# Masks of seven attention pairs put into PSUM by ScalarE copies instead of TensorE products, with PSUM banks of their own for scores

## Chip, core and metric

The kernel runs on one core of a Trainium2 chip. The metric is the device time of one execution in microseconds (us), as the median of several runs. PE is the matmul engine (TensorE), PEld its weight loads, DVE is VectorE, ACT is ScalarE, POOL is GpSimd, SP the engine that issues nearly all DMAs.

## What is computed

Windowed attention, then a gated layer, then a soft mixture of experts, all in float32. The change touches the attention alone, and there the mask:

```python
scores = scale * np.matmul(q, k.transpose(0, 1, 3, 2))      # 4 batches, 8 heads, 576 positions, 64 wide
mask_plain = (rel >= 0) & (rel < 32)                        # heads 0 to 3
mask_dil = (rel >= 0) & (rel < 128) & (rel % 4 == 0)        # heads 4 to 7
scores = np.where(masks, scores, -1e9)
attn = softmax(scores);  x = attn @ v                       # then x to (2304, 512)
x = (sigmoid(x @ w_gate) * (x @ w_val)) @ w_out             # 512 -> 1536 -> 512
...                                                         # dispatch, 8 experts, combine
```

## The kernel before

**Units and pairs.** Attention is cut into 20 units, four pairs of heads for each of five blocks of tokens (blocks 0 to 3 have 512 tokens, block 4 has 256). The four units of block 0 are done at the start (`first_attn`). The other 16 are done two at a time, as pairs 0 to 7 of the class `Pairs`, between the products of the gated layer (`l1`, matmul at L526) for blocks 0 and 1. A "half" is one call of the inner loop of `l1`: 12 matmuls of 128x512 into one bank. `Pairs` is called once after every half; `SCORES_AT` says after which half the scores of a pair are issued (1, 8, 15, 22, 27, 32, 37, 41), `TURN` how many halves later its two units are turned, and `SUMS_AT` when the weighted sums follow.

**One pair.** `scores` takes two PSUM banks. In each, one matmul of an identity with the mask (bf16, `mask_at`, L139, 128x512) opens the accumulation and writes 0 or a large negative number in every place; 128 small matmuls (L144, 64x64, in all four 32-row strips) then add query times key to it. `softmax` reads the banks on DVE (L355 maxima, L359 or L367 differences), takes exponentials on ACT, sums on DVE, and scales on POOL (L387). `turn` transposes each unit on PE (`tr`, L187) and ACT copies it to SBUF (L188). `sums` makes 128 small products with the values (L207).

**PSUM.** Eight banks: two for `l1` (`ps_l1`), two for small things (`ps_m`), four in the pool `ps_a`, handed out in turn under one tag "a": score banks, turned units (`tr`), turned output weights (`wt_ps`, L467), turned gates (`tp` in `Post.turn`, L815), and later others. A tile waits until the reader of the tile four places earlier in the ring is done.

**Order.** `tc.keep_in_program_order` (`kept`) holds instructions in the written order; for the others a planner chooses the order on each engine. Every engine takes its own queue in order. The queries and keys of pair p+1 are loaded by SP after the scores of pair p; for pair 7 the load goes into the buffers in which the units of pair 6 (block 4) keep their probabilities, so it follows their turns.

Of the kernel before, what the change touches and what calls it, by code (L numbers as in the profile page):

```python
# [17 lines left out]
P = 128  # L18
# [13 lines left out]
C0 = 21  # L32
SCORES_AT = (1, 8, 15, 22, 27, 32, 37, 41)
TURN = 4
SUMS_AT = (10, 17, 25, 29, 34, 39, 44, 47)
C1 = 19
WP = 1
ND = 4
# [21 lines left out]
def tile_kernel(  # L60
# [16 lines left out]
    ps_l1 = ctx.enter_context(tc.tile_pool(name="ps_l1", bufs=2, space=PSUM))  # L77
    ps_a = ctx.enter_context(tc.tile_pool(name="ps_a", bufs=4, space=PSUM))
    ps_m = ctx.enter_context(tc.tile_pool(name="ps_m", bufs=2, space=PSUM))

    BUFS = {
        "xa": 2, "xb": 2, "ga": 3, "gb": 3, "w": 2, "l2": 2,
# [39 lines left out]

    def keep_busy(count):
        if "ps" not in busy:
            busy["ps"] = ps_a.tile([P, 512], F32, tag="a", name="busy")
        for _ in range(count):
            kept(
                nc.tensor.matmul(
                    busy["ps"], lhsT=msk[:, M_ID:M_COLS], rhs=msk[:, 0:512], start=True, stop=True, skip_group_check=True
                )  # L130
            )
# [21 lines left out]
    def scores(u, ts):  # L153
        n, hp = u["id"]
        if "s_ps" not in u:
            u["s_ps"] = [ps_a.tile([P, 4, 64], F32, tag="a", name=f"s_ps{r}") for r in range(2)]
            for r in range(2):
                mask_at(u["s_ps"][r].rearrange("p t c -> p (t c)"), mask[:, 1 if hp >= 2 else 0])
        for t in ts:
            for i in range(4):  # L160
                for r in range(2):
                    score(u, t, i, r, u["s_ps"][r][32 * i : 32 * i + 32, t, :])
# [19 lines left out]

    def turn_unit(u, pool, tag, at=lambda x: x):
        s = u["s"].rearrange("p (c x) -> p c x", c=4)
        tr = pool.tile([P, 4, P], F32, tag=tag, name="tr")
        for c in range(4):
            at(nc.tensor.transpose(tr[:, c], s[:, c], ident))  # L187
        nc.scalar.copy(pt_ring[:, u["z"] % 4].rearrange("p c i q -> p c (i q)"), tr)  # L188
# [105 lines left out]
    class Pairs:  # L294


        def __init__(self):
            self.jobs = [(n, hp) for n in range(1, 5) for hp in HP_ORDER]
            self.us, self.qk, self.v = unit_loads(self.jobs, ["qk"] * 16)
            self.todo = []  # L300
            for p in range(8):
                t = SCORES_AT[p]
                late = t + TURN + (p == 0)
                self.todo += [(t, self.scores, p), (late, self.turn, 2 * p), (late + 1, self.turn, 2 * p + 1)]
                self.todo += [(SUMS_AT[p], self.sums, p)]
            self.todo.sort(key=lambda x: x[0])
            self.n = 0

        def __call__(self):
# [8 lines left out]
                what(2 * p + 1)  # L318

        def turn(self, z):  # L320
            turn_unit(self.us[z], ps_a, "a", kept)

        def scores(self, p):
            two = self.us[2 * p : 2 * p + 2]
            n = two[0]["id"][0]
            bank = [ps_a.tile([P, 512], F32, tag="a", name=f"s_ps{r}") for r in range(2)]
            for r in range(2):
                m_ = mask[:, 0:2] if n < 4 else mask[:, 2:3].to_broadcast([P, 2, 256])
                kept(mask_at(bank[r].rearrange("p (u c) -> p u c", u=2), m_))
            for y, u in enumerate(two):  # L330
                for t in range(4):
                    for i in range(4):
                        for r in range(2):
                            to = bank[r].rearrange("p (u t c) -> p u t c", u=2, t=4)
                            kept(score(u, t, i, r, to[32 * i : 32 * i + 32, y, t]))
            self.softmax(two, bank)
            self.load(self.qk, p + 1)
            if p == 0:
                self.load(self.v, 1)
# [82 lines left out]
    def store():  # L422
        while stores:
            ld(nc.sync.dma_start(*stores.pop(0)))
# [34 lines left out]
    def slot_weights(f, wo_f, lag):  # L459

        wt = pm.rearrange("p a b -> p (a b)").rearrange("p (k c x) -> p k c x", k=ND, c=2)
        at_ = {}

        def turned(c):
            wt_ps = ps_a.tile([P, ND, P], F32, tag="a", name="wt_ps")
            for kc in range(ND):
                nc.tensor.transpose(wt_ps[:, kc], wo_f[:, c, P * kc : P * kc + P], ident)  # L467
            nc.scalar.copy(wt[:, :, c], wt_ps)

        def product():  # L470
            pt_ps = ps_m.tile([P, 2, P], F32, tag="m", name="pt_ps")
            for kc in range(ND):
                nc.tensor.matmul(
                    pt_ps[32 * kc : 32 * kc + 32], lhsT=phi[:, kc, :], rhs=wt[:, kc], start=True, stop=True
                )
            at_["pt"] = cpool.tile([P, 2, P], F32, tag="pt", name="pt")
            nc.vector.tensor_copy(at_["pt"], pt_ps)
# [182 lines left out]
    def pair_l1(f, prev, follow):  # L660
# [14 lines left out]
        tm = b8("l2", [P, 3, 512], F32, "tm")  # L675
        m1, u2, e5 = (tm[:, z] for z in range(3))
        pn = ps_l1.tile([P, 512], F32, tag="l1", name="pa")
        pd = ps_a.tile([P, 512], F32, tag="a", name="pd")
        pe = ps_a.tile([P, 512], F32, tag="a", name="pe")
        product(pn, w["a11"], "b11", True)  # L680
        kp(nc.scalar.copy(m1, pn))
        if prev:
# [69 lines left out]
    class Post:  # L752
# [52 lines left out]
        def turn(self, q, j):  # L805
            if j == 0:
                if not self.last:
                    self.gt[q] = b8("l2", [P, self.ntt, 512], F32, "gt")
                elif q == 0:
                    ring = b8("w", [P, 2, 2, 512], F32, "gt")  # L810
                    self.gt = {z: ring[:, z % 2] for z in range(3)}
            pool, tag = (ps_l1, "l1") if self.last and j else (ps_a, "a")
            tp = pool.tile([P, 4, P], F32, tag=tag, name="tp")
            for c in range(4):
                nc.tensor.transpose(tp[:, c], g_sb[self.n, 4 * q + c][:, P * j : P * j + P], ident)  # L815
            to = self.gt[q][:, j].rearrange("p (c x) -> p c x", c=4)
# [167 lines left out]
    for f in range(NF):  # L984
        whl = split_w(wst[f // 2][:, f % 2])
        if f % 2:
            load_w(f // 2 + 2)
        l1(1, f, whl, beside)
        if NF + f in wo_at:
            convert(NF + wo_at[NF + f])  # L990
    store()
    early[0] = False
    wst.clear()
# [114 lines left out]
        st_ps.rearrange("p k (e a) -> p k e a", a=4),  # L1108
    )
    keep_busy(2)  # L1110
    h_ps = [ps_a.tile([P, 512], F32, tag="a", name=f"h_ps{h}") for h in range(2)]
    reuse = [None, None, "v", "v", "xb", "xa", "xa", "bd", "ga", "ga", "ga", "gb", "gb", "gb"]
    for e in range(8):
        for h in range(2):
# [49 lines left out]
            ALU.max,  # L1164
        )
    sr = cpool.tile([P, 512], F32R, name="sr")
    so_ps = [ps_a.tile([P, 256], F32, tag="a", name=f"so_ps{dh}") for dh in range(2)]

    def half(dh):
        return so[:, 256 * dh : 256 * dh + 256], sr[:, 256 * dh : 256 * dh + 256]  # L1170
# [30 lines left out]
    def result(dh, z):  # L1201
# [6 lines left out]
        for j in range(0, ntt, 2):  # L1208
            more = k == 4 if dh == 0 else n_op[0] // 2 % 2
            n_op[0] += dh  # L1210
            pool, tag = (ps_a, "a") if more else (ps_l1, "l1")
            op = pool.tile([P, 2, 256], F32, tag=tag, name="op")
            for y in range(2):
                kept(nc.tensor.matmul(op[:, y], lhsT=ct[:, j + y], rhs=sr_, start=True, stop=True))
            if j == 0:
# [134 lines left out]
```

## Time and profile before

| | |
|---|---|
| median of 3 runs | 499.2 us (498.91 to 499.81) |
| profiled execution, its own time | 500.05 us |
| its span from first to last instruction | 498.3 us |
| PE busy / PEld / DVE / ACT / POOL | 94% / 72% / 61% / 49% / 32% |
| chain that ended last, share of PE | 82% |

A busy share says how long an engine had an instruction in flight; for PE, matmuls overlap, so their durations add up to more than the time that they take. The chain follows the last instruction back through what released it. Only time on that chain, or in an idle stretch of the engine that it runs on, can be gained.

### The profile page before, as it was taken

What the parts mean: (1) busy time and instruction counts of PE and PEld (TensorE: products, weight loads), DVE (VectorE), ACT (ScalarE), POOL (GpSimd) and SP (SyncE); (2) the same over time, 40 slices, a digit from 0 to 9 for tenths busy, and PEclk for the clock granted to TensorE, in tenths of its full rate; (3) what the DMA queues carried; (4) which work ended last, traced back from release to release, by engine and by line L of the source; (5) the groups of instructions that cost most, each with busy time, mean ns of one, the idle gap of its engine ahead of it and who ended that gap; (6) DMA issues with size and microseconds to landing.
All of it is one profiled execution on the core that took longest, in us unless ns stands there. A gap on an engine that the chain in (4) does not pass through costs nothing.

```text
span 498.3 us, 12720 instructions
## 1 busy us (share of the span) xinstructions
PE 469.7 (94%) x5470; PEld 357.4 (72%) x5476; DVE 305.7 (61%) x567; ACT 245.4 (49%) x422; POOL 159.8 (32%) x132
## 2 busy tenths in 40 slices
PE   6789999999899999989989999999999999999993
PEld 3467777878677877867547888888887889743552
DVE  3869697976766352652997656656558655541522
ACT  2466576747666453551865554554527544300232
POOL 0243555635283421173144323324312123110100
PEclk9889999999999999999999999999999999999998
DMA  8979899979977401650002201201499886589997
GB/s 331 405 250 343 297 323 321 337 267 364 410 256 234 174 1 50 227 220 1 1 0 85 85 22 64 84 8 78 155 375 422 326 337 244 195 314 369 420 388 219
DMA packets 23785, 112.14 MB, mean 225 GB/s; under 512 B 2352, under 2 KB 7216, under 8 KB 14640
## 3 DMA queue, kind: packets, MB, share of 16 engines
q1 hardware_dynamic: 23408, 111.06, 60.0%
q8 instruction: 43, 0.70, 0.6%
q10 hardware_dynamic: 320, 0.26, 0.2%
q14 instruction: 14, 0.11, 0.1%
HBM read 97.16 MB, written 14.16 MB: 223 GB/s over the span
## 4 chain that ended last, share of the span: by engine, by line
PE 82%; DVE 7%; ACT 3%; DMA 2%; issue 2%; POOL 1%; SPq 0%; DVEq 0%; ACTq 0%; POOLq 0%
PE l1ps L526 31%; PE pa L650 12%; PE pe L650 6%; PE tp L815 4%; PE xp L207 4%; PE so_ps L1175 3%; PE h_ps L1116 3%; PE s_ps L144 3%; PE pd L650 3%; PE sp L846 2%; PE lt_ps L779 2%; DMA qk<-qkv 2%; PE tr L187 2%; PE wt_ps L467 1%; DVE whl L493 1%
## 5 line engine op out<-in xcount | busy, mean ns | idle before, releaser
L526 PE MATMUL l1ps<-x_hi,whl 128*128 128x512 f32 x384 | 129.1, 402 | 2.7 <-ACT x_hi L228 2.0
L526 PEld LDWEIGHTS l1ps<-x_hi,whl 128*128 128x128 f32 x384 | 72.1, 189 | 19.4 <-ACT x_hi L228 2.7
L526 PE MATMUL l1ps<-x_lo,whl 128*128 128x512 f32 x192 | 76.2, 397 | 0.0
L441 POOL TENSOR_TENSOR fw<-fw 128x512 int32<-128x512 int32 x36 | 51.5, 1437 | 72.4 <-DVE fw L440 35.3
L538 DVE TENSOR_TENSOR g<-l1ps,g 128x512 f32<-128x512 f32 (+1 forms) x36 | 21.6, 600 | 32.8 <-PE l1ps L526 31.5
L526 PEld LDWEIGHTS l1ps<-x_lo,whl 128*128 128x128 f32 x192 | 36.5, 190 | 7.3 <-issue 0.4
L526 PE MATMUL l1ps<-x,whl 128*128 128x256 f32 x288 | 37.0, 285 | 0.0
L526 PEld LDWEIGHTS l1ps<-x,whl 128*128 128x128 f32 x288 | 35.3, 191 | 2.0 <-issue 1.7
L536 ACT ACTIVATE g<-l1ps 128x512 f32<-128x512 f32 (+1 forms) x36 | 18.9, 526 | 31.1 <-PE l1ps L526 30.9
L493 POOL TENSOR_TENSOR whl<-w,whl 128x512 fp32r<-128x512 f32 x12 | 15.9, 1327 | 51.4 <-ACT whl L492 39.9
L815 PE MATMUL tp<-cst,g 128*128 128x128 f32 x216 | 29.2, 276 | 0.1
L493 POOL TENSOR_TENSOR whl<-wst,whl 128x512 fp32r<-128x512 f32 x12 | 16.1, 1342 | 39.0 <-ACT whl L492 33.4
L815 PEld LDWEIGHTS tp<-cst,g 128*128 128x128 f32 x216 | 24.0, 140 | 5.6 <-issue 3.3
L438 ACT ACTIVATE fw<-st 128x512 f32<-128x512 f32 x36 | 22.6, 672 | 7.0 <-DMA st<-wd 6.8
L493 DVE TENSOR_TENSOR whl<-fw,whl 128x512 fp32r<-128x512 f32 x24 | 21.4, 897 | 7.5 <-ACT whl L492 7.0
L820 ACT COPY gt<-tp 128x512 f32<-128x512 f32 x27 | 15.6, 582 | 19.1 <-PE tp L815 17.5
L207 PEld LDWEIGHTS xp<-pt_ring,v 64*64 64x64 f32 x1216 | 19.7, 137 | 6.1 <-issue 4.5
L440 DVE TENSOR_SCALAR fw<-st 128x512 int32<-128x512 uint32 x36 | 21.9, 635 | 2.8 <-DMA st<-wd 2.8
L492 ACT CAST whl<-fw 128x512 fp32r<-128x512 f32 x24 | 14.7, 620 | 17.9 <-POOL fw L441 13.6
L714 DVE TENSOR_TENSOR tm<-pe,tm 128x512 f32<-128x512 f32 x12 | 8.3, 691 | 23.7 <-PE pe L650 23.7
L439 DVE TENSOR_SCALAR fw<-fw 128x512 uint32<-128x512 uint32 x36 | 21.4, 602 | 2.3 <-ACT fw L438 1.8
L207 PE MATMUL xp<-pt_ring,v 64*64 64x32 f32 (+1 forms) x1216 | 21.1, 221 | 1.6 <-issue 0.9
(464 smaller groups left out, 968.2 us busy)
## 6 DMA issues: line engine op xcount, KB each, us to landing
ew<-w SPq DMA_DIRECT2D x32, 1024.0 KB, 8.3
st<-wd SPq DMA_DIRECT2D x18, 1024.0 KB, 9.0
wst<-wg SPq DMA_DIRECT2D x12, 1024.0 KB, 6.8
v<-qkv SPq DMA_DIRECT2D x20, 512.0 KB, 6.4
wg<-fw SPq DMA_DIRECT2D x12, 512.0 KB, 7.6
w<-wg SPq DMA_DIRECT2D x6, 1024.0 KB, 8.3
qk<-qkv SPq DMA_DIRECT2D x10, 576.0 KB, 5.7
qk<-qkv SPq DMA_DIRECT2D x8, 528.0 KB, 4.4
```

What stands on the lines that cost most here:

```text
L207: nc.tensor.matmul(o, lhsT=v[k, t, i, r, :], rhs=p_[k, 2 * r + t, i, 0:nq], start=True, stop=True)
L438: nc.scalar.activation(top, st[:, c, 1].bitcast(F32), AF.Prelu, scale=2.0**-112, alpha=2.0**32)
L439: nc.vector.tensor_scalar(top.bitcast(U32), top.bitcast(U32), 3, None, ALU.logical_shift_left)
L440: nc.vector.tensor_scalar(low.bitcast(I32), st[:, c, 0], 2.0**-29, None, ALU.mult)
L441: nc.gpsimd.tensor_tensor(low.bitcast(I32), top.bitcast(I32), low.bitcast(I32), ALU.add)
L493: (nc.gpsimd if pool[h] else nc.vector).tensor_tensor(whl[:, 1, h], src[:, h], whl[:, 0, h].bitcast(F32), ALU.subtract)
L526: nc.tensor.matmul(pt[:, 0:nt], lhsT=whl[:, w_, a, dc, :], rhs=x_[n][:, dc, :], start=first, stop=(dc == HP_ORDER[-1] and w_ == 1),)
L536: nc.scalar.activation(g, pt[:, 0:nt], AF.Sigmoid)
L538: nc.vector.tensor_tensor(g, pt[:, 0:nt], g, ALU.mult)
L650: nc.tensor.matmul(pt, lhsT=w[:, w_, P * c : P * c + P], rhs=x_[:, c], start=first and c == 0 and w_ == 0 and x_ is hi, stop=c == 1 and w_ ...
L815: nc.tensor.transpose(tp[:, c], g_sb[self.n, 4 * q + c][:, P * j : P * j + P], ident)
L820: nc.scalar.copy(to, tp)
```

## The change

Pair 0 keeps its two mask matmuls. For pairs 1 to 7 a new step `seed` runs two halves (`SEED = 2`) before the scores: it takes the two banks and issues two ACT copies of the mask (bf16 in SBUF) into them; these copies are not held in order. `scores` then only adds its 128 small matmuls. The four banks of `ps_a` become two tags of two banks: "s" for scores, "a" for turned tiles. Up to the end of block 1 (`four[0]` is False) `bank()` always hands out "a"; after that it alternates between both tags, so that four banks go round again. The units of block 0 take "a" and "s" by turns.

```diff
+SEED = 2
+    four = [False]
+    turn_ = [0]
+    def bank(shape, name):
+        turn_[0] += four[0]
+        return ps_a.tile(shape, F32, tag="as"[turn_[0] % 2], name=name, bufs=2)
@@ def scores(u, ts):            # block 0
-            u["s_ps"] = [ps_a.tile([P, 4, 64], F32, tag="a", name=f"s_ps{r}") for r in range(2)]
+            tag = "as"[u["z"] % 2]
+            u["s_ps"] = [ps_a.tile([P, 4, 64], F32, tag=tag, name=f"s_ps{r}", bufs=2) for r in range(2)]
@@ class Pairs
-                self.todo += [(SUMS_AT[p], self.sums, p)]
-            self.todo.sort(key=lambda x: x[0])
+                self.todo += [(SUMS_AT[p], self.sums, p), (t if p == 0 else t - SEED, self.seed, p)]
+            self.todo.sort(key=lambda x: (x[0], x[1] != self.seed))
+        def seed(self, p):
+            n = self.jobs[2 * p][0]
+            self.banks[p] = [ps_a.tile([P, 512], F32, tag="s", name=f"s_ps{r}", bufs=2) for r in range(2)]
+            for r in range(2):
+                to = self.banks[p][r].rearrange("p (u c) -> p u c", u=2)
+                m_ = mask[:, 0:2] if n < 4 else mask[:, 2:3].to_broadcast([P, 2, 256])
+                if p == 0:
+                    kept(mask_at(to, m_))
+                else:
+                    nc.scalar.copy(to, m_)
         def scores(self, p):
-            bank = [ps_a.tile([P, 512], F32, tag="a", name=f"s_ps{r}") for r in range(2)]
-            for r in range(2):
-                m_ = mask[:, 0:2] if n < 4 else mask[:, 2:3].to_broadcast([P, 2, 256])
-                kept(mask_at(bank[r].rearrange("p (u c) -> p u c", u=2), m_))
+            bank = self.banks.pop(p)
...
@@ turn_unit, slot_weights, Post.turn, pair_l1, expert stage: ps_a.tile(.., tag="a") becomes bank(..)
@@ after the last half of block 1
+    four[0] = True
     store()
```

## Rows read from the trace of the kernel before

**Rows 1.** Busy time by stretches: start:end, length, then each engine's busy us (instructions), PE clock, DMA share.

```profile
75.00:100.00 25.00, 25.00 (x355) 20.31 (x354) 22.32 (x36) 17.77 (x28) 15.21 (x11) 1.00 0.96 330
...
50.00:193.00 143.00, 139.71 (x2138) 112.19 (x2139) 98.51 (x165) 85.34 (x132) 68.47 (x52) 1.00 0.73 260
```

**Rows 2.** Waits of PE from 50 to 217 us: total us, times, longest.

```profile
PE s_ps L144 <- issue: 2.4, 2, 1.6
PE tr L187 <- POOL sm L387: 0.7, 1, 0.7
PE l1ps L526 <- ACT g L536: 0.7, 1, 0.7
PE s_ps L144 <- DMA qk<-qkv: 0.6, 1, 0.6
```

**Rows 3.** Instructions on the score banks, 24 to 217 us: duration ns min/median/max, first and last start.

```profile
L139 PE MATMUL s_ps<-msk x15: 379/379/390, 35.6 to 193.5; 128*128 128x512 bf16 x15
...
L367 DVE TENSOR_TENSOR qk<-s_ps,mx x8: 415/415/415, 179.8 to 209.7; 128x256 f32<-128x256 f32 x8
```

**Rows 4.** Timeline of PE at pairs 1 and 6: start us, us, operation.

```profile
56.46 0.39 PE L526 MATMUL l1ps<-x_hi,whl 128*128 128x512 f32 x1
56.69 0.60 PE L139 MATMUL s_ps<-msk 128*128 128x512 bf16 x2
57.23 1.49 PE L144 MATMUL s_ps<-qk 64*32 64x64 f32 x128
...
176.17 0.60 PE L187 MATMUL tr<-cst,sm 128*128 128x128 f32 x4
176.61 0.59 PE L139 MATMUL s_ps<-msk 128*128 128x512 bf16 x2
177.13 1.48 PE L144 MATMUL s_ps<-qk 64*32 64x64 f32 x128
```

**Rows 5.** PE at pair 7, and the transfer on the chain there.

```profile
193.25 0.59 PE L139 MATMUL s_ps<-msk 128*128 128x512 bf16 x2
193.78 2.81 PE L779 MATMUL lt_ps<-g,wp 128*32 128x128 f32 x90
197.17 0.86 PE L144 MATMUL s_ps<-qk 64*32 64x64 f32 x64 [0.58 <-DMA qk<-qkv]
...
193.56 3.57 DMA qk<-qkv
```

**Rows 6.** Event semaphores on PE's queue before L526.

```profile
L526 PEldq EVENT_SEMAPHORE  x2: 51/51/51, 58.5 to 96.9; - x2
```

**Rows 7.** Turned tiles at the end of block 1, on PE and on ACT.

```profile
217.08 0.66 PE L187 MATMUL tr<-cst,qk 128*128 128x128 f32 x4 [1.35 <-POOL qk L387]
217.57 1.04 PE L815 MATMUL tp<-cst,g 128*128 128x128 f32 x8
...
217.77 0.59 ACT L188 COPY pt_ring<-tr 128x512 f32<-128x512 f32 x1 [1.14 <-PE tr L187]
```

**Rows 8.** The two breaks inside scores, counts up to each, and PE's instruction queue.

```profile
129.55 0.33 PE L144 MATMUL s_ps<-qk 64*32 64x64 f32 x11 [1.59 <-issue]
...
154.42 0.31 PE L144 MATMUL s_ps<-qk 64*32 64x64 f32 x7 [0.79 <-issue]
...
0.00:129.53 129.53, 117.24 (x2006) 90.47 (x2009) 97.97 (x174) 74.87 (x119) 56.04 (x45) 0.97 0.90 327
0.00:154.40 154.40, 141.32 (x2388) 109.38 (x2392) 113.39 (x201) 89.63 (x142) 68.66 (x54) 0.98 0.89 322
...
q8 instruction: 43, 0.70, 0.6%
```

**Rows 9.** ACT: groups of copies with mean ns of one, and its longest wait there.

```profile
L492 ACT CAST whl<-fw 128x512 fp32r<-128x512 f32 x22 | 13.5, 620 | 17.4 <-POOL fw L441 13.2 <-PE l1ps L526 4.0
...
L188 ACT COPY pt_ring<-tr 128x512 f32<-128x512 f32 x16 | 9.3, 583 | 5.5 <-PE tr L187 5.5
...
ACT pt_ring L188 <- PE tr L187: 5.5, 4, 3.1
```

More of the change, by code (lines that the diff above doesn't have):

```diff
@@ L124, in keep_busy @@
         if "ps" not in busy:
-            busy["ps"] = ps_a.tile([P, 512], F32, tag="a", name="busy")
+            busy["ps"] = bank([P, 512], "busy")
         for _ in range(count):
@@ L184, in turn_unit @@
         s = u["s"].rearrange("p (c x) -> p c x", c=4)
-        tr = pool.tile([P, 4, P], F32, tag=tag, name="tr")
+        tr = pool.tile([P, 4, P], F32, tag=tag, name="tr") if pool else bank([P, 4, P], "tr")
         for c in range(4):
@@ L304, in __init__ @@
                 self.todo += [(t, self.scores, p), (late, self.turn, 2 * p), (late + 1, self.turn, 2 * p + 1)]
-                self.todo += [(SUMS_AT[p], self.sums, p)]
-            self.todo.sort(key=lambda x: x[0])
+                self.todo += [(SUMS_AT[p], self.sums, p), (t if p == 0 else t - SEED, self.seed, p)]
+            self.todo.sort(key=lambda x: (x[0], x[1] != self.seed))
+            self.banks = {}
             self.n = 0
@@ L320, in turn @@
         def turn(self, z):
-            turn_unit(self.us[z], ps_a, "a", kept)
+            turn_unit(self.us[z], None, None, kept)
+        def seed(self, p):
[8 more added lines that the diff above has]
+                    nc.scalar.copy(to, m_)
         def scores(self, p):
@@ L464, in turned @@
         def turned(c):
-            wt_ps = ps_a.tile([P, ND, P], F32, tag="a", name="wt_ps")
+            wt_ps = bank([P, ND, P], "wt_ps")
             for kc in range(ND):
@@ L677, in pair_l1 @@
         pn = ps_l1.tile([P, 512], F32, tag="l1", name="pa")
-        pd = ps_a.tile([P, 512], F32, tag="a", name="pd")
-        pe = ps_a.tile([P, 512], F32, tag="a", name="pe")
+        pd = bank([P, 512], "pd")
+        pe = bank([P, 512], "pe")
         product(pn, w["a11"], "b11", True)
@@ L811, in turn @@
                     self.gt = {z: ring[:, z % 2] for z in range(3)}
-            pool, tag = (ps_l1, "l1") if self.last and j else (ps_a, "a")
-            tp = pool.tile([P, 4, P], F32, tag=tag, name="tp")
+            shape = [P, 4, P]
+            tp = ps_l1.tile(shape, F32, tag="l1", name="tp") if self.last and j else bank(shape, "tp")
             for c in range(4):
@@ L1110, in tile_kernel @@
     keep_busy(2)
-    h_ps = [ps_a.tile([P, 512], F32, tag="a", name=f"h_ps{h}") for h in range(2)]
+    h_ps = [bank([P, 512], f"h_ps{h}") for h in range(2)]
     reuse = [None, None, "v", "v", "xb", "xa", "xa", "bd", "ga", "ga", "ga", "gb", "gb", "gb"]
@@ L1166, in tile_kernel @@
     sr = cpool.tile([P, 512], F32R, name="sr")
-    so_ps = [ps_a.tile([P, 256], F32, tag="a", name=f"so_ps{dh}") for dh in range(2)]
+    so_ps = [bank([P, 256], f"so_ps{dh}") for dh in range(2)]
     def half(dh):
@@ L1210, in result @@
             n_op[0] += dh
-            pool, tag = (ps_a, "a") if more else (ps_l1, "l1")
-            op = pool.tile([P, 2, 256], F32, tag=tag, name="op")
+            shape = [P, 2, 256]
+            op = bank(shape, "op") if more else ps_l1.tile(shape, F32, tag="l1", name="op")
             for y in range(2):
```

## The prediction

> **What bounds the kernel now.** I read the page first for the chain that ended last: PE holds most of it, and scores and layer products lie on it one after the other. The mask products can only matter where their neighbours are PE work too, so I went to the table by stretches. The change lies between the first scores of a pair and the last, 35 to 217 us. From 50 to 193 us PE is busy 139.7 of 143.0 us, from 75 to 100 us all 25.0, at a granted clock of 1.00, which is the upper level of 2.4 GHz [rows 1]. ACT is busy 85.3 of 143.0 us, so 57.7 are free. The view of waits says what PE's few idle stretches are: twice "issue" inside scores (2.4 us in all), once POOL's scaling ahead of a turn, once a sigmoid that frees a layer bank, once the keys of a pair by DMA, 0.6 to 0.7 us each [rows 2]. Nothing else ends a wait of PE. So in this stage the order on PE is the time, and an instruction taken off PE is worth what it occupies there, unless what follows it is late for another reason. After 217 us the chain goes on through PE, and what is early there starts the later loads early as well.
>
> **What a mask product occupies.** The group of L139 gives 379 ns for one [rows 3]. 12 of these (pairs 1 to 6) would be 4.5 us, but that is the wrong price: the durations overlap. At pair 1 the last layer product starts at 56.46, the masks at 56.69, the scores at 57.23 us [rows 4]. The row of two masks is 0.60 us long; less one duration of 0.38 it leaves 0.22 between their starts. So the two take 0.44, and 0.10 of the 0.54 up to the scores is the change from a full-width product to the small ones. That change does not go away, since the scores then follow a layer product or a turn, which are full-width too. At pair 6 the masks start at 176.61 and the scores at 177.13, 0.52, of the same make [rows 4]. I take 0.44 for each pair; the bound is 0.53, if the change costs nothing behind a turn, and below that nothing. The page "TensorE: Matmul & The Clock Gate" of the Trainium skill, section "Back-to-back issue gap", gives N/2.4 + 2.5 ns, 216 ns for 512 columns. By it the 12 products are 2.6 us, by the group's durations 4.5; the starts in the timeline agree with the page.
>
> Pairs 1 to 6: 6 x 0.44 = **2.6 us** saved (up to 3.2).
>
> **Pair 7 saves nothing.** Its masks run from 193.25 us, then come logits of the finished block as filler, and then PE waits 0.58 us for keys: the transfer starts at 193.56, right after the turn of the first unit of pair 6, and takes 3.57 us, to 197.13 [rows 5]. The turn lies ahead of the masks, so without them the filler ends 0.44 earlier and the wait is 1.0 instead of 0.58. I take 0, bound 0.53.
>
> **What the seeds cost on ACT.** 14 copies of 128x512 from SBUF into PSUM. The trace has none in that direction; the nearest are the casts SBUF to SBUF at 620 ns and the copies PSUM to SBUF at 583 ns [rows 9]. 14 x 0.60 = 8.4 us. ACT's 57.7 idle us hide them, hence cost 0; with that cover gone they would cost up to 8.4. A seed can wait for one thing, DVE's last reading of the same banks for the pair before. The closest case is pair 7: seeds after half 39, scores of pair 6 after half 37; those are read from 179.8 us on by L367, eight in all for pairs 6 and 7 at 0.415 [rows 3]; four end at 181.5, and two halves of 2.8 after the start of the scores at 177.13 it is past 182 [rows 4]. Behind a seed on ACT stand sigmoids and copies of turned units, and PE's banks wait for these.
>
> **The new wait.** The first score of each unit group now waits for ACT, where it used to follow a product of its own engine. The seed is issued two halves ahead: a half is 12 products 0.23 apart [rows 4], 2.76 us, so the copy has 5.5 us for 1.2 us of work, and ACT's longest wait for a turn is 3.1 us [rows 9]. 3.1 + 1.2 fits in 5.5. What remains is bookkeeping: scores already wait for DMA, and an instruction with a second wait gets an event semaphore ahead of it, 51 ns on PE's queue [rows 6]. I take one for each of six pairs, **0.3 us** lost; bounds 0 and 0.6.
>
> **Two banks for turned tiles instead of four.** Three such tiles within about a microsecond now make the third wait for the ACT copy of the first. Along the pairs, turns and turned weights are some halves apart and their copies follow within a microsecond. At the end of block 1 they crowd: a turn at 217.08, then two `tp` from 217.57 on, and the copy of the turn from 217.77 to 218.36 [rows 7]. The second `tp` began about 218.0 (four of the eight transposes later) and can now start at about 218.4: 0.4 us. The same pattern stands once more one half later. Layer products, which are not held in order, can be put ahead, so between 0 and 0.8; I take **0.4 us** lost. From block 1's end on, alternating tags of two banks are a ring of four again: nothing. The same holds for block 0's units, whose score banks alternate in twos as they did. The loads that `scores` issues stay behind the scores.
>
> **The breaks in scores.** PE stops 1.59 us after 117 of 128 products of pair 4, and 0.79 us after 121 of pair 5, with nothing late. Before the first break the rows count 4015 instructions on PE, before the second 4780, 765 apart, three times 255. PE's instructions come in 43 packets of 0.70 MB together, 16.3 KB each [rows 8]; 255 instructions for each is 64 bytes an instruction. So I read these breaks as ends of a packet inside a dense block, where the next had not come. Each pair loses four instructions (two products, two weight loads): at pair 4 the end moves 16 instructions on, to product 125, at pair 5 20, past the last. If the next packet comes at the same clock time as before, what these two pairs save is waited out: 0.9 lost. If the ends fall harmlessly, 2.4 are gained. I take 0, as most dense blocks hold such an end without a break.
>
> **Sum.** -2.6 + 0.3 + 0.4 = -1.9 us. Made against the profiled execution: 500.05 (span 498.3 and 1.75 around it) to 498.15. That execution is 0.85 over the median of the runs, so the median goes from 499.2 to **497.3 us**. With the terms' bounds: at best 6 x 0.53 + 0.53 + 2.4 = 6.1 saved, 493.1; at worst, without a rival, 2.6 - 0.6 - 0.8 - 0.9 = 0.3 saved, 498.9.
>
> **Rivals.** *Something else is late (499.2).* Pair 7 shows the pattern: PE arrives earlier and waits longer. It becomes the rule if the weights for block 0, which pass DMA, ACT, DVE and POOL, are just in time. For it: from 75 to 100 us DMA is at 0.96 and DVE busy 22.3 of 25 [rows 1]. Against it: PE is busy all 25 us there, so nothing came late, and most of that chain is started by PE freeing buffers, so it moves along. It decides once two thirds of the 2.6 are waited out.
>
> *ACT's queue (slower, 500.8).* The copies are free to be placed by the planner. A seed ahead of a sigmoid delays the bank that the half after next needs; of the 2.76 us of a half the read takes about 0.6, so from 2.1 us of lateness on PE stands. An exponential and its table load together with two seeds would reach that. If each of the seven pairs exposes one copy, 7 x 0.6 = 4.2 are lost against 2.6 saved: 500.8; both copies, 505.0. For it: PE already waited once for a sigmoid [rows 2]. Against: ACT has 40% free. The page "TensorE: Matmul & The Clock Gate", "Specifications", says that ScalarE's queue is strictly first in, first out, where TensorE can pull weight loads ahead; this speaks against moving work from PE to ACT. By it no later sigmoid passes a seed that waits. The trace agrees that ACT stands up to 3.1 us at one instruction [rows 9].
>
> *The breaks go (494.9).* The 1.9 and 2.4 more, less what else shifts: 4.3. For it, the wait on the banks ahead of the masks goes, so PE's queue can be filled earlier; against, the end at pair 4 stays inside the scores.
>
> **How the numbers follow.** Forecast as summed 0.52 (its own range 496.0 to 498.9); something else late 0.18; ACT's queue 0.15; breaks gone 0.15. A measurement of this kernel tells about 0.2%, 1.0 us, from no change. Faster: 0.52 less 0.04 for its upper end, the 0.15 of the breaks, and 0.04 of the "late" case: 0.67. Same: 0.14 of the late case, 0.04 of the forecast, 0.01 of ACT's: 0.19. Slower: 0.14. The range leaves out about half of the case of the breaks and a little under half of ACT's: 495.0 to 500.5.
>
> **What the changed profile would show.** L139 keeps two matmuls of pair 0 and eight of block 0. Scores of pairs 1 to 6 start about 0.32 us after the start of the last layer product ahead of them (0.23 and 0.10). Fourteen ACT copies into `s_ps` of about 0.6 us end over 2 us before their scores. The wait for keys at pair 7 grows to about 1.0 us. The `tp` behind a turn near 215 us starts late or behind layer products. From 50 to 193 us the same work is about 2.6 us shorter. I would be wrong if PE shows waits for `s_ps` on ACT, new waits of L526 for a sigmoid or for weights, or breaks by "issue" of another length than 2.4 us in all: each us there shifts the sum by one.

## The result, and the profile after

The changed kernel takes 504.7 us (median of 6 runs, 502.1 to 507.0), the kernel before beside it 499.1 (6 runs): ratio 1.0089, 95% interval 1.0065 to 1.0114. The ratio is worth 4.4 us, the two medians are 5.6 us apart, and the repetition below gives 4.0; I reckon with 4. The kernel is slower, and outside the predicted range of 495.0 to 500.5 us. Its profiled execution is its fastest: 502.09 us, span 499.9, only 1.6 over the span of before, whose profiled execution lies 0.85 us above its median.

First what the edit did where it was made. The score banks in the changed kernel (duration min/median/max in ns, first and last start):

```profile
L345 ACT CAST s_ps<-msk x14: 575/588/610, 44.4 to 181.9; 128x512 f32<-128x512 bf16 x14
...
L147 PE MATMUL s_ps<-msk x1: 379/379/379, 36.3 to 36.3; 128*128 128x512 bf16 x1
...
  ACT s_ps L345: 6.1, 3
```

Fourteen copies of 0.59 us have taken the place of the products; pair 0's one visible product is left. The last row stands under "who waited for it": ACT stood 6.1 us at three of the copies. At pair 1 the scores follow the last layer product by 0.32 us, where 0.77 us lay between them [rows 4]:

```profile
56.72 0.39 PE L547 MATMUL l1ps<-x_hi,whl 128*128 128x512 f32 x1
57.04 1.19 PE L152 MATMUL s_ps<-qk 64*32 64x64 f32 x99
...
129.59 0.31 PE L152 MATMUL s_ps<-qk 64*32 64x64 f32 x5 [2.16 <-issue]
...
216.26 0.66 PE L196 MATMUL tr<-cst,qk 128*128 128x128 f32 x4 [1.73 <-POOL qk L408]
216.75 0.60 PE L836 MATMUL tp<-cst,g 128*128 128x128 f32 x4
217.28 1.04 PE L867 MATMUL sp<-gt,dt 128*32 128x512 f32 x2
218.26 0.66 PE L836 MATMUL tp<-cst,g 128*128 128x128 f32 x4
218.85 1.06 PE L867 MATMUL sp<-gt,dt 128*32 128x512 f32 x6
219.84 0.50 PE L547 MATMUL l1ps<-x_hi,whl 128*128 128x512 f32 x1
```

The same timeline shows two things that were not in the sum. The break inside pair 4's scores is now 2.16 us (1.59 before, [rows 8]; pair 5's is gone). At the end of block 1 the order is another than in [rows 7]: turn, one `tp`, one gather product `sp` (dispatch weights times turned gates), one `tp`, three `sp` (each `sp` counts as two rows here). Before, turn, two `tp` and four `sp` followed one another. Four `sp` side by side, each on 32 columns of the array, took 1.06 us before; now one alone takes 1.04 and the other three again 1.06.

The second `tp` stands apart because it waits for a bank. Its weight load on PE, and the copy on VectorE that reads the first `tp` out of its bank:

```profile
218.26 0.42 PEld L836 LDWEIGHTS tp<-cst,g 128*128 128x128 f32 x4 [0.84 <-DVE gt L839]
...
217.39 0.69 DVE L839 COPY gt<-tp 128x512 f32<-128x512 f32 x1 [2.08 <-PE tp L836]
```

and that copy in the kernel before, where the second `tp` had begun at about 218.0 [rows 7], ahead of it:

```profile
218.21 0.69 DVE L818 COPY gt<-tp 128x512 f32<-128x512 f32 x1 [2.08 <-PE tp L815]
```

PE's waits from 50 to 217 us, to be held against [rows 2]:

```profile
PE s_ps L152 <- issue: 2.2, 1, 2.2
PE tr L196 <- POOL qk L408: 1.7, 1, 1.7
PE dt_ps L846 <- DVE x L424: 0.8, 1, 0.8
PE s_ps L152 <- DMA qk<-qkv: 0.8, 1, 0.8
```

The waits for `x`, and the longer one for POOL's scaling, are both behind pair 7, between 210 and 216 us.

To place the difference, three more names: `wst` is a 1 MB block of layer weights that comes by DMA, `whl` what ACT casts from it for the layer products, and `h_ps` takes the first products of the experts. I counted the starts of layer products on PE's timeline, twelve to a half, and took differences, so that a late or early start of the program drops out. "Fetch" is the start of the packet of the instruction queue nearest to the first load of `wst` for the pair stage (issued at 202.82 us before), "cast" the first cast into `whl` after it, both from that issue on; the last column goes from the last first-layer half to the first product into `h_ps`. All kernels of this study, one profiled execution each, in us:

```
                  half     half     half     fetch   cast    half     half 71
                  2 to 31  31 to 44 44 to 47                 60 to 66 to h_ps
before            110.11   64.19    16.34    -1.9    6.24    10.69    18.62
after             109.87   61.96    19.04    +3.2    7.63    11.08    19.38
after_again       109.71   62.16    19.13    +4.2    7.69    11.49    19.37
banks_only        112.81   63.44    17.81    -1.9    6.53    11.08    20.96
no_masks          108.46   61.87    18.86    +3.1    7.53    11.08    21.06
seeds_kept        108.73   62.14    19.04    +4.4    7.62    11.08    19.37
one_ring          109.01   62.46    19.24    +3.2    7.59    10.77    20.31
one_ring_kept     112.09   62.26    17.82    +3.3    7.72    11.55    18.62
seeds_tail        108.89   62.26    19.16    +3.3    7.73    10.70    18.61
tail_hoisted      109.76   63.47    16.46    -2.0    6.58    11.14    19.37
after_pad         115.06   61.96    17.67    -1.6    6.25    11.08    19.37
one_ring_pad      111.09   62.34    16.35    -2.0    6.24    10.70    18.61
seeds_tail_pad    109.27   61.89    17.81    -2.3    6.36    10.75    18.61
before_less       112.61   63.30    17.62    +3.0    7.52    10.70    18.62
after_late_pad    109.69   62.79    17.80    -2.1    6.40    11.08    19.37
before_late_pad   110.36   63.92    16.36    -2.7    6.27    10.75    18.62
best_no_pad       110.84   62.14    18.18    +4.5    7.78    10.76    18.61
best              112.30   62.78    16.68    -2.1    6.25    12.10    18.62
```

Before against after: 2.5 us are gained up to half 44 (most of it between 31 and 44), 2.7 are lost in the three halves behind it, 0.4 and 0.75 in the last two columns. That is the 1.6 of the spans, with 0.3 from the start. One profile each is little: the first column alone runs from 108.5 to 115.1.

### The profile page after: what moved, and what is told of

It is laid out like the page before. It is cut to its first block, busy times and chain, and to the rows that moved or that the text cites. A ratio compares the mean times of both kernels' runs of the same rounds, so it can differ in the third digit from the quotient of the medians.

```text
span 499.9 us, 12714 instructions
## 1 busy us (share of the span) xinstructions
PE 467.9 (94%) x5456; PEld 355.6 (71%) x5462; DVE 308.9 (62%) x567; ACT 251.8 (50%) x436; POOL 158.1 (32%) x132
## 4 chain that ended last, share of the span: by engine, by line
PE 67%; DVE 6%; ACT 4%; DMA 3%; issue 2%; POOL 1%; SPq 0%; DVEq 0%; ACTq 0%
PE l1ps L547 22%; PE pa L671 12%; PE pe L671 6%; PE tp L836 3%; PE h_ps L1138 3%; PE pd L671 3%; PE sp L867 3%; PE so_ps L1197 2%; PE lt_ps L800 2%; PE xp L216 2%; DMA v<-qkv 1%; PE s_ps L152 1%; PE wt_ps L488 1%; DVE t_hl L574 1%; PE tr L196 1%
## 5 line engine op out<-in xcount | busy, mean ns | idle before, releaser
L460 DVE TENSOR_SCALAR fw<-fw 128x512 uint32<-128x512 uint32 x36 | 22.4, 630 | 3.9 <-ACT fw L459 3.3
L514 DVE TENSOR_TENSOR whl<-fw,whl 128x512 fp32r<-128x512 f32 x24 | 22.8, 963 | 2.8 <-ACT whl L513 2.3
L461 DVE TENSOR_SCALAR fw<-st 128x512 int32<-128x512 uint32 x36 | 20.7, 600 | 2.8 <-DMA st<-wd 2.8
L513 ACT CAST whl<-wst 128x512 fp32r<-128x512 f32 x24 | 14.0, 619 | 15.2 <-PE l1ps L547 7.9
```

The lines of the kernel that those rows point to most:

```text
L460: nc.vector.tensor_scalar(top.bitcast(U32), top.bitcast(U32), 3, None, ALU.logical_shift_left)
L461: nc.vector.tensor_scalar(low.bitcast(I32), st[:, c, 0], 2.0**-29, None, ALU.mult)
L514: (nc.gpsimd if pool[h] else nc.vector).tensor_tensor(whl[:, 1, h], src[:, h], whl[:, 0, h].bitcast(F32), ALU.subtract)
```

## The experiments

Five rounds each, against the kernel before on the same chip, which gave 500.1 to 500.5 us.

**The change again, and its parts.** after_again is the changed kernel unedited.

> The changed kernel once more, for a second profile and to see how far its runs lie apart. Its first runs gave 502.1 to 507.0 us, its profile was of the fastest. All theories: median 503 to 506. The queue theory (the planner puts the copies into ScalarE's queue as soon as it believes the bank free; in the first profile ScalarE stood 6.1 us before three of them) expects ScalarE to stand 4 to 12 us before copies into s_ps again, and TensorE to lose its time between 60 and 110 us. The rival that the two-bank ring of turned tiles costs it expects the loss near turned tiles, after 110 us.

504.2 us, 1.0083 [1.0056, 1.0110]; its profile repeats the table's pattern. The net loss lies behind half 44, and not between 60 and 110 us as the queue theory had it.

banks_only: the banks kept apart, the masks by products as before.

```diff
-                self.todo += [(SUMS_AT[p], self.sums, p), (t if p == 0 else t - SEED, self.seed, p)]
+                self.todo += [(SUMS_AT[p], self.sums, p), (t, self.seed, p)]
...
-                if p == 0:
-                    kept(mask_at(to, m_))
-                else:
-                    nc.scalar.copy(to, m_)
+                kept(mask_at(to, m_))
```

> Masks by products as before, at the time of the scores, but score banks and turned tiles in two tags of two banks. Ring theory: 502 to 505, most of the loss is here. Queue theory: 498.5 to 500.5, no measurable change, since ScalarE has nothing new to do.

505.3 us, 1.0074 [1.0039, 1.0110]: about as the ring theory has it. Without any copy by ScalarE the kernel is about as slow as the whole change.

no_masks: pairs 1 to 7 get no mask, neither product nor copy; each of their score products opens a sum of its own.

```diff
-                else:
-                    nc.scalar.copy(to, m_)
...
-            start=False,
+            start=start,
```

> Pairs 1 to 7 get no mask at all (left out of the computation): neither products nor copies, every score product opens its own accumulation; banks as in the changed kernel. Queue theory: 495.5 to 498, the 2 to 3 us that the products took and nothing lost on ScalarE. Rival, that the planner's new order on VectorE and TensorE (it differs as soon as the products go) costs the time: 501 to 505, as VectorE's order here is nearly that of the changed kernel.

502.8 us, 1.0043 [1.0018, 1.0068]. With the masks gone at no price, still slower than before: something other than the masks' cost is lost.

seeds_kept: the copies are held at their written place in ScalarE's queue (`kept(nc.scalar.copy(to, m_))`).

> The changed kernel with the copies held in the written order, so that they stand two halves ahead of their scores in ScalarE's queue and not right behind the exponential of the pair before. Queue theory: no wait of ScalarE before a copy into s_ps, 496 to 499. Rival (the copies' 8.4 us of ScalarE work themselves, or the planner's order): 502 to 505, as the changed kernel.

503.2 us, 1.0052 [1.0023, 1.0081], 1.0 us under after_again. The two intervals overlap, and the 496 to 499 of the queue theory are missed: the place of the copies is at most a part. The changed kernel's ScalarE, with the planner free to place the copies:

```profile
86.81 0.59 ACT L345 CAST s_ps<-msk 128x512 f32<-128x512 bf16 x1 [2.34 <-DVE sm L380]
87.33 0.68 ACT L459 ACTIVATE fw<-st 128x512 f32<-128x512 f32 x1
88.03 1.28 ACT L395 ACT_TABLE_LOAD   x1
89.33 1.06 ACT L395 ACTIVATE sm<-sm 128x1024 f32<-128x1024 f32 x1
```

and with them held:

```profile
84.64 1.28 ACT L395 ACT_TABLE_LOAD   x1
86.94 1.06 ACT L395 ACTIVATE sm<-sm 128x1024 f32<-128x1024 f32 x1 [1.02 <-DVE sm L380]
```

The copy for the next pair stood ahead of the exponential of this one and waited 2.34 us for VectorE's reading of the same banks. VectorE's last difference (L380) released copy and exponential alike: with the copies free the exponential began 2.5 us after that (89.33, released by 86.81), with the copies held at once (86.94), its table load done during the wait. The sigmoid and the casts of layer weights queued behind it are late with it. Halves 2 to 31 take 108.73 us with the copies held, 109.87 without: 1.1 us. The rule of the Trainium skill that the prediction named, that ScalarE's queue is strictly first in, first out ("TensorE: Matmul & The Clock Gate", the table of specifications at its head), is what these two pieces show.

My theory from here (A): the split of the pool in two tags costs, since it changes the order that the planner writes. If so, ScalarE's copies in the old ring of four must be a gain.

**The copies without the split.** one_ring: all tiles of that pool back in one tag of four.

```diff
-        return ps_a.tile(shape, F32, tag="as"[turn_[0] % 2], name=name, bufs=2)
+        return ps_a.tile(shape, F32, tag="a", name=name)
...
-            self.banks[p] = [ps_a.tile([P, 512], F32, tag="s", name=f"s_ps{r}", bufs=2) for r in range(2)]
+            self.banks[p] = [ps_a.tile([P, 512], F32, tag="a", name=f"s_ps{r}") for r in range(2)]
```

In this kernel and the two that share its ring the copied masks do not all count in the scores; the time is that of the same instructions. (The Trainium skill, "PSUM — Partial Sum Buffer", "PSUM: the matmul accumulator", says that only TensorE changes the marks by which a product adds or overwrites, and that a product which opens a sum clears them for its whole bank region; by this rule the copies need banks that no other product opens, and these kernels are tests, not a remedy. No run here shows the marks.)

> The other half of the change alone: ScalarE copies the masks of pairs 1 to 7 two half steps early, but scores, turned tiles and all others stay in the one ring of four banks that the kernel before has, so that the order written at the end of block 1 and in the tail is that of before. Theory A (the split of the pool into two tags is what costs): the 2 to 4 us that the pairs save up to 212 us stay, the stretch from the last first-layer half to h_ps takes 18.6 us again and not 19.4, and the ratio to before is 0.992 to 0.997 (496 to 498). Rival B (the copies in ScalarE's queue cost, whatever the banks): 1.004 to 1.009, as the change itself. Rival C (products and copies weigh the same, the rest is the clock): 0.999 to 1.002.

501.4 us, 1.0023 [1.0005, 1.0040]: above the 0.992 to 0.997 of theory A.

> As the run before it, with the copies held at their written place in ScalarE's queue, behind the work of the half steps ahead of them. Theory A: 0.990 to 0.996, since the wait of ScalarE for the softmax ahead of early copies (6.1 us in the changed kernel) is gone too; rival B: if only the early place of the copies costs, 0.994 to 0.998 here and over 1.002 in the run with the copies free. Rival C: 0.999 to 1.002.

502.9 us, 1.0036 [1.0012, 1.0061]. Theory A falls as the whole cause. PE's order at block 1's end and in the tail was that of before, the tail's last column 18.6 in the second, and yet the three halves behind half 44 lost 1.5 and more.

seeds_tail and tail_hoisted try the tail from both sides. The first edit below, on top of the held copies, is seeds_tail; the second, in the kernel before, is tail_hoisted.

```diff
+            at = kept if self.last and q == 0 and j == 0 else (lambda x: x)
             for c in range(4):
-                nc.tensor.transpose(tp[:, c], g_sb[self.n, 4 * q + c][:, P * j : P * j + P], ident)
+                at(nc.tensor.transpose(tp[:, c], g_sb[self.n, 4 * q + c][:, P * j : P * j + P], ident))
```

```diff
-                [(self.logits,)]
+                (t[:1] if last else [])
+                + [(self.logits,)]
...
-                + t[: k + half]
+                + t[last : k + half]
```

> The changed kernel with the copies held in written order, and the first turned gate tile of the last block held behind the filler products, as before had it. Theory A: the stretch from the last first-layer half to h_ps takes 18.6 us and no longer 19.4 to 21, the clock stays above 0.95 at 437 to 446 us, and the time is 1 to 2.5 us under that of the kernel with only the copies held: ratio to before 0.998 to 1.003. Rival (the tail's order is beside the point): 1.005, as with the copies held alone.

502.3 us, 1.0045 [1.0018, 1.0072]: the stretch is 18.61 us again as theory A has it, but the whole is no better than its rival said (1.005), and 0.9 us under seeds_kept is not clear of noise.

> The kernel before, masks by products and one ring, with one thing of the changed kernel: the first turned gate tile of the last block stands ahead of its logits. Theory A: the stretch to h_ps takes 0.8 us more in each execution and up to 2.5 more where the clock drops after the idle time: ratio 1.001 to 1.005. Rival: 0.999 to 1.001.

501.1 us, 1.0022 [1.0008, 1.0036]. One turned tile moved in the old kernel costs 1.1 us. PE and ScalarE there:

```profile
432.85 0.27 PE L826 MATMUL dt_ps<-cst,d 64*128 64x64 f32 x1 [0.69 <-ACT d L804]
...
434.36 0.38 PE L749 MATMUL wcol<-cst,t 1*128 1x1 f32 x2 [0.60 <-ACT t L744]
...
430.49 0.59 ACT L821 COPY gt<-tp 128x512 f32<-128x512 f32 x1 [3.07 <-DVE nm L799]
431.10 1.28 ACT L800 ACT_TABLE_LOAD   x1
432.39 0.20 ACT L800 ACTIVATE nm<-nm 64x1 f32<-64x1 f32 x1
432.50 0.29 ACT L804 ACTIVATE d<-d 64x128 f32<-64x128 f32 x1
```

and the same place with the tile held (seeds_tail):

```profile
426.88 1.28 ACT L820 ACT_TABLE_LOAD   x1
429.92 0.21 ACT L820 ACTIVATE nm<-nm 64x1 f32<-64x1 f32 x1 [1.76 <-DVE nm L819]
431.05 0.31 ACT L824 ACTIVATE d<-d 64x128 f32<-64x128 f32 x1 [0.92 <-DVE d L823]
...
432.27 0.60 PE L837 MATMUL tp<-cst,g 128*128 128x128 f32 x4
433.04 0.38 PE L770 MATMUL wcol<-cst,t 1*128 1x1 f32 x2 [0.17 <-ACT t L765]
```

With the tile held, the table load for the exponential stands in ScalarE's idle time and the last four transposes fill PE's time until `wcol` can start. With the tile hoisted its work sits 0.4 us earlier (the column of halves 60 to 66), a copy stands ahead of the table load, and PE waits twice (0.69 and 0.60 us). The changed kernel has the same two waits there, 0.69 and 0.61.

**The fetch.** With the tail settled, at least 1.3 us behind half 44 were without a cause in the one-ring kernels. The table has it: in all kernels up to here whose mask products are gone, the cast into `whl` comes 7.5 to 7.8 us after the issue of the load instead of 6.2 to 6.6. What the cast waited for, in the kernel before, in the changed kernel, and in before_less (below):

```profile
209.06 1.14 ACT L492 CAST whl<-wst 128x512 fp32r<-128x512 f32 x2 [1.79 <-DMA wst<-wg]
...
208.26 1.14 ACT L513 CAST whl<-wst 128x512 fp32r<-128x512 f32 x2 [3.18 <-DMA wst<-wg]
...
213.70 1.14 ACT L492 CAST whl<-wst 128x512 fp32r<-128x512 f32 x2 [3.08 <-DMA wst<-wg]
```

The transfers of the kernel before, first the stretch ahead of that issue, then from the issue to the cast (queue: packets, MB, share):

```profile
q8 instruction: 1, 0.02, 3.1%
...
q1 hardware_dynamic: 363, 2.14, 90.1%
```

and of the changed kernel from the issue, at 200.63 us, to the cast:

```profile
q1 hardware_dynamic: 437, 2.39, 90.2%
q8 instruction: 1, 0.02, 0.8%
```

In the kernel before the one packet of the instruction queue, 16 KB in 0.98 us, came before the load; now it falls 3.2 us into it. By the list of packets the last ones of `wst` then end one behind another, 0.31 us apart, until 7.1 us after the issue, where all had ended by 5.8 before. I read this as one transfer engine that is a microsecond late, and the load with it; the list does not name the engine of a packet. The change took 28 instructions off PE (14 products, 14 weight loads), and so a packet's end comes 28 instructions later in the program (theory F). The first test puts them back at the program's start, or takes them from the kernel before:

```diff
-SMALL = 70
+SMALL = 84
```

(`SMALL` counts the tiny products at the program's start; it is 58 in before_less.)

> The changed kernel with 14 more of the tiny idle products (28 instructions of TensorE) that stand at its start, while TensorE waits for the first load: they take the places of the 28 instructions that the change took away, so that every 16 KB packet of TensorE's instructions after pair 7 is fetched at the point of the program where the kernel before fetched it. Theory F (the fetch's place costs): in the kernel before, the fetch near 201 us began 1.9 us ahead of the issue of the load of wst and the cast into whl began 6.2 us after that issue; in the changed kernel the fetch falls 3 to 4 us into the load and the cast begins 7.6 us after. Here the fetch is ahead of the load again, the cast comes 6.2 to 6.6 us after the issue, TensorE's wait for pair 7's weights is about 1.35 us and not 1.75, and the time is 1 to 2.5 us under the changed kernel's: ratio to before 1.004 to 1.006. Rival (the place of the fetch is beside the point): cast 7.6 us after the issue, ratio 1.008 to 1.009.

508.6 us, 1.0148 [1.0103, 1.0193].

> ScalarE's copies in the one ring of four banks, with the same 28 instructions at the start. (With one ring the copied masks do not all stand in the scores of this kernel and of the run without these instructions, since turned tiles pass through the same banks: it computes other weights with the same instructions.) Theory F: cast 6.2 to 6.6 us after the issue of the load, the 2.6 us that are gained up to 212 us are kept, ratio 0.994 to 0.998. Rival: 1.002 as without them.

503.6 us, 1.0065 [1.0045, 1.0085].

> Copies held in written order and the last block's first turned tile held behind the filler, with the same 28 instructions at the start. Theory F: ratio 0.999 to 1.002, with the split of the four gather products at block 1's end still to pay (1 us). Rival: 1.0045 as without them.

502.6 us, 1.0050 [1.0028, 1.0073].

> The kernel before with 12 fewer of the tiny idle products at its start (24 instructions of TensorE), nothing else: at the load of wst near 203 us the fetch stands where the changed kernel has it. Theory F: fetch 3 to 4 us after the issue of the load, cast into whl 7.4 to 7.7 us after it in place of 6.2, and the kernel is slower by 1 to 2.5 us: ratio 1.002 to 1.005. Rival: 0.999 to 1.001.

506.5 us, 1.0130 [1.0098, 1.0161]. At the place itself theory F is right in all four: fetch ahead of the load and cast at 6.2 to 6.4 us in the three, fetch 3.0 us into it and cast at 7.52 in the kernel before with 24 instructions fewer, whose three halves go from 16.34 to 17.62. The whole times missed: the same instructions moved all stages before, by up to 5 us in halves 2 to 31, where DMA is near its limit [rows 1]. How they act there I did not take apart.

So the next pair puts 28 instructions just ahead of pair 6's first turn, and changes nothing earlier.

```diff
+        if at is kept and u["z"] == 12:
+            for i in range(14):
+                at(nc.tensor.matmul(tr[0:32, 0, 0:32], lhsT=msk[:, 0:32], rhs=msk[:, 0:32], start=True, stop=True))
         for c in range(4):
             at(nc.tensor.transpose(tr[:, c], s[:, c], ident))
```

> The changed kernel with 28 instructions of TensorE (14 products of 32x32 that the transposes behind them overwrite) ahead of pair 6's first turned tile, near 190 us, and nothing changed before that. Theory F: the fetch comes about 2 us ahead of the issue of the load of wst, the cast into whl 6.2 to 6.6 us after it, and the stretch from half 44 to half 47 of the first layer takes 17.7 us and not 19.0; with some 0.5 us for the products themselves the time is 0.5 to 1.5 us under the changed kernel's: ratio 1.005 to 1.008. Rival (fetch beside the point): 19.0 us, ratio 1.009 to 1.010.

503.0 us, 1.0058 [1.0035, 1.0081]: 28 instructions of work added, and 1.2 to 1.7 us under the changed kernel. Cast at 6.40, three halves 17.80.

> The kernel before with the same 28 instructions at the same place: the price of the products alone. The fetch moves from 1.9 us ahead of the load to some 4 to 6 ahead, the cast stays 6.2 to 6.6 us after the issue, the stretch from half 44 to 47 stays 16.3 to 16.5 us; 0.3 to 0.8 us slower, ratio 1.0005 to 1.002. If any move of the fetch costs, 1.003 or more.

500.1 us, 1.0001 [0.9988, 1.0015]: they cost nothing that shows. The fetch moved only from 1.9 to 2.7 us ahead of the load (4 to 6 were expected), without effect.

**The gather products, and all together.** best_no_pad is seeds_tail with the four `sp` held together; best adds the 28 instructions.

```diff
-                nc.tensor.matmul(
+                ins = nc.tensor.matmul(
                     sp[32 * j : 32 * j + 32],
...
+                if self.n == 0 and q == 0:
+                    kept(ins)
```

> Copies held in written order, the last block's first turned tile held behind the filler, and the four gather products of block 0 at block 1's end held together. If the split of the products into 1 and 3 costs the other half of the loss, the stretch from half 44 to 47 takes 17.6 to 17.9 us and not 19.1: 1.0 to 1.3 us under the run without that hold, ratio 1.001 to 1.003. If not, 19.1 us and 1.0045.

500.5 us, 1.0013 [0.9989, 1.0038]. The three halves go from 19.16 to 18.18 (17.6 to 17.9 were expected).

> As the run before it, with the 28 instructions ahead of pair 6's first turned tile: all three causes away. If they are all, the stretch from half 44 to 47 takes 16.3 to 16.8 us, the one from the last first-layer half to h_ps 18.6 us, and the 3 to 3.6 us gained up to half 44 are kept: span 494.5 to 496.5, ratio 0.993 to 0.998. If executions with a lower clock stay as frequent as in the changed kernel whatever the order, 0.999 to 1.002.

501.1 us, 1.0016 [0.9992, 1.0041]. Three halves 16.68, tail 18.62, as forecast, but the whole is no faster than before: it falls into the second branch of what was expected. Against seeds_tail_pad this execution lost 3.0 us in halves 2 to 31 and 1.4 in halves 60 to 66, where PE waited 0.35 and 0.45 us for `whl`, which I did not follow up. The break of pair 4 took 2.35 us, and behind it PE's granted clock was 0.50 (columns as in [rows 1]):

```profile
130.41 0.43 PE L152 MATMUL s_ps<-qk 64*32 64x64 f32 x6 [2.35 <-issue]
...
131.00:133.00 2.00, 2.00 (x13) 1.22 (x6) 2.00 (x4) 0.01 (x1) 0.00 (x0) 0.50 1.00 399
```

## Why the prediction was wrong

The masks did go from PE at about their price. Four other terms were wrong: the copies on ACT (0 in the sum, 1.0 us measured), two banks at block 1's end (0.4, measured 1.35), the tail (0, measured 1.1) and the instruction fetch at a load (not in the sum, 1.3). They come to 4.8 us, where the sum had 0.4.

**The saving of pairs 1 to 6, 2.6 us: near in size, by luck in part.** From half 2 to half 44 the changed kernel gained 2.5 us. With the copies held the same stretch gained 3.4, without any mask (no_masks) 4.0, so the 2.5 are a larger saving less what the copies cost. Nor is it 0.44 a pair: 0.2 came up to half 31 and 2.2 behind it, where pair 5's break of 0.79 also went. Up to half 31, about 1 was lost to early copies and 0.6 to the longer break at pair 4.

**"From block 1's end on, alternating tags of two banks are a ring of four again: nothing": this step failed.** In the changed kernel the planner put a turned tile of the last block ahead; with all tiles in one tag again (one_ring, one_ring_kept) it did not. So I read it that banks in two tags no longer force the tiles' order. tail_hoisted shows the price alone: 1.1 us (0.45 and 0.75 in the table's last two columns; other stretches of that profile were shorter), on a chain where ScalarE's table load had been hidden.

**Two banks at block 1's end, 0.4 us: the right place, a third of the size.** The second `tp` does wait for a bank, but for VectorE's copy of the first `tp` and not, as the prediction has it, for ACT's copy of the turn. The prediction let layer products fill such a wait. The planner put one `sp` into it, and the other three then cost a second 1.06 us. With the fetch out of the way, three halves take 17.7 to 17.8 us split and 16.3 to 16.5 unsplit: 1.35. best_no_pad and best got 1.0 to 1.1 of it back by the hold of the four. There layer products do fill the wait, and some 0.3 us is left of it (16.68 for three halves against 16.36 in before_late_pad); in best:

```profile
219.90 0.42 PEld L840 LDWEIGHTS tp<-cst,g 128*128 128x128 f32 x4 [0.29 <-DVE gt L843]
```

**The fetch, absent from the sum: 1.3 us.** I had read the packets of instructions and counted where their ends move, but asked only about breaks inside scores. That a moved packet meets a load was not asked. The gain before half 44 does not matter to it; the load is 1.3 us late wherever the packet falls into it (before_less, and all kernels without mask products except the padded ones), and pair 7's exponential, PE's wait for the turn (1.35 to 1.73) and the next halves follow.

**ACT's copies, 0: about 1.0 us** (1.1 in halves 2 to 31, 1.0 between the medians, which alone is not clear of noise). The duration was right (588 ns for 600). "The copy has 5.5 us for 1.2 us of work" took the copy's own deadline; it should have asked what stands behind it. It was the rival by ACT's queue at about a quarter of its price, and the exponential, not the sigmoid, was late.

**Breaks, 0: right as a sum** (2.4 before, 2.2 after), and right in what they are. The list of packets shows it: in the 18 profiles there are 35 breaks by "issue" of over 0.3 us between 45 and 215 us, and each ends 1.0 to 1.5 us after a packet of PE's instructions has landed. At pair 4 the break moved on from product 117 to 123 (125 was forecast). PE came to it earlier, at 127.43 instead of 127.96 us, the packet landed at 128.23 instead of 128.09, and PE went on at 129.59 instead of 129.55: what had been gained up to there was waited out, as the prediction has it for a packet that comes at the same time as before. Event semaphores, 0.3: three stand ahead of scores, 51 ns each, 0.15 us. Pair 7's wait for keys grew from 0.58 to 0.76 us, and I had expected 1.0.

**The clock was not in the sum.** In one_ring PE stood 1.75 us before the turn at 215.80, and the granted clock fell from 1.00 to 0.50, that is from 2.4 to 1.2 GHz; so it did again in the tail. One_ring by stretches (start:end, length, busy us of PE, PEld, DVE, ACT, POOL, PE clock, DMA share):

```profile
214.00:215.80 1.80, 0.05 (x1) 0.00 (x1) 0.85 (x1) 1.35 (x2) 1.80 (x3) 1.00 0.07 27
216.00:219.00 3.00, 3.00 (x16) 2.34 (x19) 0.69 (x1) 1.01 (x2) 3.00 (x3) 0.50 0.87 330
442.00:444.00 2.00, 2.00 (x16) 0.63 (x12) 0.00 (x0) 0.00 (x0) 0.00 (x0) 0.50 0.01 4
```

The 24 `si_ps` products of the tail took 4.47 us in it and 2.78 in seeds_tail; from the turn to the next layer product it took 4.07 us, one_ring_pad 2.45. So each fall cost 1.6 to 1.7 us, and a different kernel showed it at a different place: banks_only, one_ring_kept and best behind pair 4's break (2.08, 2.00 and 2.35 us), no_masks, banks_only and one_ring in the tail, after_pad and one_ring_pad elsewhere. Over its 12 executions best ran at 0.979 to 0.991; at 0.979 it took 502.6 and 503.6, at 0.989 499.3 to 500.3: 3.1 us for 0.010. The changed kernel's executions average 0.984, those of the kernel before 0.988 to 0.989; by that rate, an estimate, 1.2 to 1.5 us of the 4.

**What stays open.** 1.6 us of spans and some 1.4 by the clock leave about 1 us of the 4 that no single profile shows. best at a clock of 0.988 and over averages 499.8 us, the kernel before at such clocks 500.2; that is not the 2.8 us that the first two columns of seeds_tail (3.2 gained) and the three halves of best (0.3 lost) let expect together. Its early halves, its break and its halves 60 to 66 were longer than in seeds_tail_pad, and whether they differ so from one execution to the next was not measured. What decides when a packet of instructions starts, and with it how long a break lasts, is not shown either.

## What to carry to other kernels

On a tuned kernel with a written order, like this one, an edit has two prices: that of its instructions, and that of the order and the places of everything behind it. After such an edit compare the planner's written order engine by engine first, and lay stretch lengths from one fixed product to another side by side; then undo one difference at a time, close behind the place it acts on. Splitting a ring of buffers into tags can remove order as well as banks. Where it makes a tile wait, see what the planner puts into the wait. And work that is taken off an engine may be waited for further down, at a load that shares its time with something else.

## What the hardware showed unexpectedly

- A 16 KB packet of PE's instructions took 0.9 to 1.4 us near this load (18 profiles). Where it fell into a 1 MB load, the cast behind it came 7.5 to 7.8 us after the issue (nine profiles), where it came earlier, 6.2 to 6.6 (the other nine).
- Each of 35 breaks of PE inside dense work, 0.3 to 2.35 us long, ended 1.0 to 1.5 us after such a packet had landed.
- Some 24 to 28 tiny instructions more or fewer at the start of the program made kernels 0.3 (not clear of noise) to 6 us slower, in both directions; 28 near 190 us changed the kernel before by nothing that shows.
- One 32-column gather product of 512 columns takes 1.04 us alone, and four side by side 1.06.
- The tail's 24 `si_ps` products took 2.8 us at a granted clock of 1.00 and 4.47 at 0.50; whether the clock falls after a wait of some 2 us differs from one profile to the next: it fell after 1.75 us in one_ring, 2.00, 2.08 and 2.35, and stayed after 2.16 in the changed kernel and 2.08 in one_ring.
